# One pair of weights loaded in two parts: 128 rows without the last query tile, and that tile as 64-row tiles in partitions 0 to 63

## The chip, the cores and the metric

The kernel runs on one core of a Trainium2 chip. A core has five engines (TensorE, written PE; VectorE, DVE; ScalarE, ACT; GpSimd, POOL; SyncE, SP), an on-chip memory of 128 partitions, a matmul accumulator memory, and 16 DMA engines that bring data from the chip's main memory. The metric is device microseconds of one execution. The kernel before took 2490.28 us, the median of three runs between 2489.77 and 2490.39.

## The reference

Two layers, each of one attention block over a cached sequence and one token mixer, for a batch of two with one token each. Only float32 is used.

```python
x = x + A(layernorm(x)); x = x + B(layernorm(x))      # twice
def A(x):                        # x: (2, 1, 512)
    q = (x @ wq)                 # 32 query heads of 128, four to each of the 8 key heads
    scores = q . k_cache / sqrt(128)      # k_cache, v_cache: (2, 8, 32768, 128)
    return softmax(scores) @ v_cache @ wo # wo: (4096, 512)
def B(x):                        # (2, 1, 512), one token: outer products
    return gelu(x * w1 + b1) @ w2 + b2    # w1: (1, 1792), w2: (1792, 1)
```

Both caches, 268 MB each, are read once per layer, all but a few pieces that stay on the chip from one layer to the next. The weights wq and wo, 8.4 MB each, are read in head groups.

## The kernel before, in words

**Units.** A unit is one layer, one batch element and one key head: 2 x 2 x 8 = 32 units. For a unit the kernel computes the query rows of the head (`make_q`, `q_products`), loads the head's keys and multiplies them (`load_k`, `k_chunk`, L426), takes the maximum and the exponentials, loads the values and multiplies them (`load_v`, `v_chunk`, L581), and adds the result times wo (`out_0` to `out_2`). A unit's keys and values are 16 MB each, in eight chunks of 4096 positions.

**Memory.** `mem` is one on-chip tile of 13 cells of 4096 columns (2 MB over 128 partitions) and a rest of 2560 columns. In the first and the last part of the program keys and values use cells 0 to 7 as two buffers of four cells, so nearly every load is 8 MB, 128 rows of 64 KB. In the middle (from unit N1 to N3, where one layer ends and the next begins) loads are smaller and use a ring that reaches to cell 10. Cell 8 (`RING * RING - 1`) holds small work rows: `spot()` hands out one of its eight places of 512 columns, in rotation. Cells 9 to 12 hold weights.

**Weights.** Heads go in pairs (`TWO_HEADS`): (0, 1), (2, 3), (4, 6), (5, 7). `load_weights` (L114 to L118) brings a pair by one load of 4096 KB, 128 rows of 32 KB, on SyncE's queue, into cells 9 and 10 or 11 and 12. A head's part is four query tiles (`wq_at`, 128 rows x 512 columns each, one for each quarter of the 512 inputs) and four output tiles (`wo_at`). The pairs that are not resident are loaded once in each layer, seven loads in all. `q_products` (L340) makes the query row of a head as four products of 128 inputs each, `q_ps[n] += xnT[:, d, b].T @ wq_at(h)[:, d, :]`, d = 0 to 3.

**Order.** One loop at the end walks through the loads in the order of `stream`; after each chunk it runs what has been booked for that moment with `at(time, f, ...)`, where time counts chunks. The program order of each engine follows from this. All large loads are issued by SyncE, one after the other; each waits until TensorE has used what stood in its buffer. `at(kbeg[n] - 10, load_weights, ...)` books a pair's load ten chunks before the keys of its first head begin.

Of the kernel before, what the change touches and what calls it, by code (L numbers as in the profile page):

```python
# [13 lines left out]
P = 128  # L14
CK = 4096
# [5 lines left out]
RING = 3  # L21
# [23 lines left out]
def gqa_mixer_kernel(ctx: ExitStack, tc: tile.TileContext, x, kt, v, wqo, cols, out):  # L45
# [17 lines left out]
    nc = tc.nc  # L63
    B, D = out.shape
# [4 lines left out]
    R = wqo.shape[2] // (4 * D)  # L69
    DT = D // P  # L70
    FT = (cols.shape[1] - 1) // 4
# [16 lines left out]
    widths |= dict(selh=R, mask=QT, others=B, oz=2 * R * B, qpads=NP, unit=2 * 16, ln=16 + 2 * FT)  # L88
# [20 lines left out]
    def wq_at(h):  # L109
        return cells(home[h])[:, :W].rearrange("p (t c) -> p t c", t=DT)  # L110

    def wo_at(h):
        return cells(home[h])[:, W:].rearrange("p (t c) -> p t c", t=R)

    def load_weights(k, cell):
        for j in range(2):
            home[TWO_HEADS[k][j]] = cell + j
        nc.sync.dma_start(cells(cell, 2), wqo[k])  # L118


    busy = [0] * 2 * (WCELL0 + WCELLS + 1)
    now = [0]
# [72 lines left out]
    ident = sm["ident"]  # L195
# [84 lines left out]
    N1 = len(units) - 1  # L280
# [5 lines left out]
    N3 = len(units) - 1  # L286
# [7 lines left out]
    xnT = sm["xn"].rearrange("p (d b) -> p d b", b=B)  # L294
# [26 lines left out]
    def unit_of(n):  # L321

        return units[n]

    q_ps, q_row, q_kept = {}, {}, {}
# [7 lines left out]
    def q_products(n, *ds):  # L333

        layer, b, h = unit_of(n)
        m = 1 if partner(n) is None else B
        for d in ds:
            if d == 0:
                q_ps[n] = bcast if N1 < n <= N3 + 2 else kept[0]
            nc.tensor.matmul(  # L340
                q_ps[n][:m, :],
                xnT[:, d, b : b + m],
                wq_at(h)[:, d, :],
                start=(d == 0),
                stop=(d == DT - 1),
            )

    def make_q(n, step, place=None):

# [339 lines left out]
    ln = sm["ln"]  # L689
# [238 lines left out]
    kbeg, k_done, vbeg, v_done, vend_of, v_from, v_to, brings, starts, t = {}, {}, {}, {}, {}, {}, {}, [], [], 0  # L928
# [13 lines left out]
    def at(time, f, *a, rank=1):  # L942
        done.setdefault(time, []).append((rank, f, a))

    HC = NCH // HALVES
    opens = {two[0]: k for k, two in enumerate(TWO_HEADS)}
    mixed = {}
    for n in range(NU):
        layer, b, h = unit_of(n)
# [19 lines left out]
                assert max(v_done[n - 2, c] for c in range(HC)) <= q2  # L969
        if n and h in opens and (units[n] == (0, 0, h) or h in passing and units[n] == (1, 0, h)):  # L970
            at(kbeg[n] - (7 if n == N3 + 2 else 10), load_weights, opens[h], WCELL0 + opens[h] % 2 * 2)
        if n in (N1 + 1, N2 + 1):
            at(kend - 0.5, turn_scores, n, 0, rank=2)
            at(kend, q_products, n + 1, 0)
            at(kend, max_1, n)
            at(kend, q_products, n + 1, 1)
            at(kend, max_2, n)
            at(kend, exponentials_at_once, n, 0)
            at(kend, q_products, n + 1, 2, 3)
            t1 = kend + 2  # L980
# [94 lines left out]
    t = 0  # L1075
# [11 lines left out]
    assert not done, sorted(done)  # L1087


def _layout(A_x, A_k_cache, A_v_cache, A_wq, A_wo, B_w1, B_b1, B_w2, B_b2):  # L1090
# [23 lines left out]
    return {  # L1114
        "x": np.ascontiguousarray(A_x.reshape(B * (D // P), P).T),
        "kt": kt,
        "v": A_v_cache.reshape(B * HKV, SK * DH),
        "wqo": np.stack([np.concatenate([wqo[h] for h in two], axis=1) for two in TWO_HEADS]),
        "cols": np.concatenate(cols, axis=1),
    }  # L1120

# [24 lines left out]
```

## Time and profile before

| | |
|---|---|
| median of three runs | 2490.28 us |
| the profiled execution | 2490.09 us |
| its span | 2488.0 us |
| bytes read | 1061.19 MB |
| granted TensorE clock | 0.772 |
| loads of weight pairs (L118) | 7 of 4096 KB |

The profile has one execution. Its span runs from the first to the last instruction that the profiler saw, 2.1 us less than the execution's own time. Lines L114 and so on are those of the kernel before; in the changed kernel the same statements stand 7 to 44 lines further down.

### The profile page before, as it was taken

To read this page: it belongs to the slowest core of one execution; us is meant where nothing else is said; L and a number is where in the kernel's file an instruction comes from. 1 tells how busy PE (TensorE), PEld (TensorE's weight loads), DVE (VectorE), ACT (ScalarE), POOL (GpSimd) and SP (SyncE) were. 2 spreads that over 40 slices of the span, in tenths; PEclk is the share of its full clock that TensorE was granted. 3 is DMA by queue.
4 is the path that set the end of the run, shared out by engine and by line. 5 is a ranking of instruction groups with operands and counts; after the bars stand their busy time and mean duration, and the time that the engine had idled before them with its cause. 6 is when DMAs were issued, how large, how long until landed. Compare 5 with 4: busy or idle time off the path is not lost.

```text
span 2488.0 us, 20543 instructions
## 1 busy us (share of the span) xinstructions
PE 1371.4 (55%) x9302; PEld 376.2 (15%) x9302; DVE 244.9 (10%) x643; ACT 187.7 (8%) x554; POOL 4.9 (0%) x17
## 2 busy tenths in 40 slices
PE   4544445544545454657677665455455465455546
PEld 1111111111111111111121121111111111111112
DVE  1000000000000000003113110000000000010002
ACT  0000000000000000002012000000000000011002
POOL 0000000000000000000000000000000000000000
PEclk8777767876777777778888887777678677777878
DMA  9999999999999999999999999999999999999996
GB/s 421 437 432 428 433 436 430 434 435 427 436 436 432 426 436 431 427 431 407 433 427 417 428 432 432 438 430 431 432 428 438 428 429 435 431 434 431 432 431 291
DMA packets 30336, 1062.51 MB, mean 427 GB/s; under 512 B 3621, under 2 KB 3625, under 8 KB 4266
## 3 DMA queue, kind: packets, MB, share of 16 engines
q1 hardware_dynamic: 29960, 1061.17, 99.1%
q8 instruction: 73, 1.20, 0.2%
q14 instruction: 13, 0.11, 0.0%
q10 hardware_dynamic: 290, 0.04, 0.0%
HBM read 1061.19 MB, written 0.00 MB: 427 GB/s over the span
## 4 chain that ended last, share of the span: by engine, by line
DMA 73%; PE 25%; DVE 1%; issue 0%; another core or an unknown queue 0%; ACT 0%; SPq 0%; POOL 0%; ACTq 0%
DMA mem<-in_v_dram 64%; PE acc L581 20%; DMA mem<-in_kt_dram 9%; PE scores L426 3%; PE small L612 0%; PE small L455 0%; PE small L449 0%; PE bcast L340 0%; ACT S L466 0%; PE small L642 0%; PE kept L246 0%; PE kept L792 0%; PE bcast L672 0%; DVE S L551 0%
## 5 line engine op out<-in xcount | busy, mean ns | idle before, releaser
L426 PE MATMUL scores<-mem,small_sb 128*32 128x512 f32 x4096 | 631.7, 736 | 605.4 <-DMA mem<-in_kt_dram 605.2
L581 PE MATMUL acc<-mem,S 128*16 128x512 f32 x4088 | 596.8, 723 | 457.1 <-DMA mem<-in_v_dram 447.7
L426 PEld LDWEIGHTS scores<-mem,small_sb 128*32 128x32 f32 x4096 | 150.0, 129 | 988.7 <-issue 903.7
L466 ACT ACTIVATE S<-S,small_sb 128x128 f32<-128x128 f32 x240 | 123.4, 517 | 2107.9 <-DVE small_sb L457 1556.9
L581 PEld LDWEIGHTS acc<-mem,S 128*16 128x16 f32 x4088 | 132.6, 109 | 810.8 <-issue 664.4
L441 DVE TENSOR_REDUCE small_sb<-scores 128x1 f32<-128x512 f32 x64 | 44.2, 691 | 819.5 <-PE scores L426 819.5
L461 DVE STREAM_TRANSPOSE S<-scores 128x512 f32<-128x512 f32 x64 | 45.5, 710 | 116.0 <-PE acc L581 116.0
L340 PE MATMUL kept<-mem,small_sb 128*2 128x512 f32 x104 | 51.1, 617 | 1.7 <-DVE small_sb L274 1.7
L466 ACT ACTIVATION_READ_ACCUMULATOR S<-S,small_sb 128x1 f32 x240 | 44.7, 186 | 0.0
L246 PE MATMUL kept<-mem,small_sb 128*1 128x512 f32 (+1 forms) x236 | 42.4, 598 | 2.6 <-ACT mem L835 2.4
L451 DVE TENSOR_REDUCE small_sb<-small 1x4 f32<-1x128 f32 x32 | 8.9, 279 | 277.7 <-PE small L449 277.7
L614 DVE RECIPROCAL small_sb<-small 128x4 f32<-128x4 f32 x32 | 5.9, 185 | 304.6 <-PE small L612 304.6
L623 DVE TENSOR_TENSOR small_sb<-small,small_sb 128x4 f32<-128x4 f32 x31 | 5.1, 164 | 295.8 <-PE small L621 295.8
L551 DVE SCALAR_TENSOR_TENSOR S<-acc,small_sb,S 128x128 f32<-128x128 f32 x93 | 32.6, 351 | 3.3
L835 ACT ACTIVATE S<-bcast,small_sb 128x512 f32<-128x512 f32 x28 | 21.5, 777 | 87.2 <-DVE small_sb L704 85.1
L366 PE MATMUL small<-small_sb,mem 2*128 2x2 f32 x112 | 15.5, 256 | 17.9 <-DVE mem L362 17.9
L549 DVE TENSOR_SCALAR S<-acc,small_sb 128x128 f32<-128x128 f32 x31 | 10.8, 350 | 147.3 <-PE acc L581 147.3
L621 PEld LDWEIGHTS small<-small_sb,S 128*128 128x128 f32 x62 | 12.7, 258 | 48.8 <-issue 41.2
L340 PE MATMUL bcast<-mem,small_sb 128*1 128x512 f32 (+1 forms) x40 | 19.4, 600 | 0.0
L366 PEld LDWEIGHTS small<-small_sb,mem 2*128 2x128 f32 x112 | 14.3, 196 | 30.5 <-DVE mem L362 27.3
L852 DVE SCALAR_TENSOR_TENSOR acc<-S,small_sb,acc 128x512 f32<-128x512 f32 x24 | 18.1, 755 | 2.5
L449 PE MATMUL small<-small_sb 128*1 128x128 f32 x64 | 16.6, 353 | 3.1 <-DVE small_sb L447 3.1
(147 smaller groups left out, 285.3 us busy)
## 6 DMA issues: line engine op xcount, KB each, us to landing
mem<-in_kt_dram SPq DMA_DIRECT2D x14, 4096.0 KB, 22.5
mem<-in_v_dram SPq DMA_DIRECT2D x11, 4096.0 KB, 29.2
mem<-in_wqo_dram SPq DMA_DIRECT2D x7, 4096.0 KB, 37.6
mem<-in_v_dram SPq DMA_DIRECT2D x13, 2048.0 KB, 21.3
mem<-in_kt_dram SPq DMA_DIRECT2D x12, 2048.0 KB, 19.3
mem<-in_kt_dram SPq DMA_DIRECT2D x24, 1024.0 KB, 8.8
mem<-in_v_dram SPq DMA_DIRECT2D x21, 1024.0 KB, 8.8
mem<-in_kt_dram SPq DMA_DIRECT2D x2, 6144.0 KB, 24.2
```

What stands on the lines that cost most here:

```text
L246: nc.tensor.matmul((rows if to is None else to)[32 * g : 32 * g + b + 1, :], weights if b else weights[:, 1:], row, start=to is not None, ...
L340: nc.tensor.matmul(q_ps[n][:m, :], xnT[:, d, b : b + m], wq_at(h)[:, d, :], start=(d == 0), stop=(d == DT - 1),)
L366: nc.tensor.matmul(pt[:, r * m : (r + 1) * m], q_row[n][:m, r * DH : (r + 1) * DH], ident[:m, :m], start=True, stop=True,)
L426: nc.tensor.matmul(sc_ps[n, half][32 * g : 32 * g + 32, :], q, kc[k * NG + g], start=(i == 0 and k == 0), stop=(i == PACK - 1 and k == SUB ...
L441: nc.vector.tensor_reduce(mx[n][:, half : half + 1], sc_ps[n, half], axis=AX.X, op=ALU.max)
L449: nc.tensor.matmul(pm[:1, :P], mxa, ident, start=True, stop=True)
L461: nc.vector.transpose(S[half], sc_ps[n, half])
L466: nc.scalar.activation(s[:, :, h], s[:, :, h], AF.Exp, bias=neg[n][:, h : h + 1], scale=SCALE, accum_out=lsum[n][:, half, h : h + 1],)
L551: nc.vector.scalar_tensor_tensor(t, acc[:, k * DH : (k + 1) * DH], mask[:, k : k + 1], t, op0=ALU.mult, op1=ALU.add)
L581: nc.tensor.matmul(acc[32 * g : 32 * g + R * QT, :], S[half][:, col : col + R * QT], vc[q], start=(c == v_from[n] and q < NG), stop=(c == ...
L835: nc.scalar.activation(hid[key, f], px[key], AF.Gelu_apprx_tanh, bias=shift[key][:, f : f + 1], scale=slope[key][:, f : f + 1],)
L852: nc.vector.scalar_tensor_tensor(h if f == FT - 1 else acc, h, w, acc, op0=ALU.mult, op1=ALU.add)
```

## The change

The pair (4, 6), number 2 of `TWO_HEADS` (`PART = 2`), is loaded in two parts. The host puts the last query tile (d = 3) of both heads apart. What is left, seven tiles for each head, goes by a load of 3584 KB (128 rows of 28 KB) to the same cells as before. The two tiles taken out, 128 rows each, are cut into an upper and a lower half of 64 rows, and the four half tiles (512 KB) go side by side to partitions 0 to 63 of cell 8, by one load of 64 rows of 8 KB on SyncE's queue, booked 28 chunks ahead of the head's keys. Both loads happen once in each layer.

[...] So `lower_input` copies the inputs 64 to 127 of the last quarter to partitions 0 to 63 (a product with half of the identity matrix and a copy by VectorE), and `q_products` makes the last product of heads 4 and 6 as two products of 64 inputs.

Since cell 8 is now used by the half tiles, `spot()` hands out work rows from the rest (five places) ahead of unit N1 and from unit N3 + 4 on, and from cell 8 only between.

```diff
+PART, LOWERED = 2, 1
...
     def load_weights(k, cell):
+        tiles = 2 * (DT + R - LOWERED * (k == PART))
         for j in range(2):
-            home[TWO_HEADS[k][j]] = cell + j
-        nc.sync.dma_start(cells(cell, 2), wqo[k])
+            home[TWO_HEADS[k][j]] = cell * CK + j * (tiles // 2) * D
+        of = wqo[k].rearrange("p c -> (p c)")[: P * tiles * D].rearrange("(p c) -> p c", p=P)
+        nc.sync.dma_start(mem[:, cell * CK :][:, : tiles * D], of)
+
+    def lower_tiles():
+        low = mem[:H, (WCELL0 - 1) * CK :][:, : 4 * LOWERED * D]
+        to = low.rearrange("u (i c) -> u i c", i=2)
+        for j in range(2):
+            lowered[TWO_HEADS[PART][j]] = [[to[:, i, (LOWERED * j + d) * D :][:, :D] for i in range(2)] for d in range(LOWERED)]
+        of = wqo[PART].rearrange("p c -> (p c)")[-H * 4 * LOWERED * D :].rearrange("(u c) -> u c", u=H)
+        nc.sync.dma_start(low, of)
+
+    def lower_input():
+        p = misc()
+        nc.tensor.matmul(p[:H, : LOWERED * B], ident[:, H:], sm["xn"][:, -LOWERED * B :], start=True, stop=True)
+        nc.vector.tensor_copy(sm["low"][:H, :], p[:H, : LOWERED * B])
...
     def spot():
         spots[0] += 1
-        return cells(RING * RING - 1)[:, spots[0] % (CK // D) * D :][:, :D]
+        inside = kbeg[N1] <= now[0] < kbeg[N3 + 4]
+        w, m = ((WCELL0 - 1) * CK, CK // D) if inside else ((WCELL0 + WCELLS) * CK, REST)
+        return mem[:, w + spots[0] % m * D :][:, :D]
...
+            j = d - (DT - LOWERED)
+            if h in lowered and j >= 0:
+                low = sm["low"][:, j * B : (j + 1) * B]
+                pairs = [(x[:H, b : b + m], t) for x, t in zip((xnT[:, d, :], low), lowered[h][j])]
+            else:
+                pairs = [(xnT[:, d, b : b + m], wq_at(h, d))]
...
             at(kbeg[n] - (7 if n == N3 + 2 else 10), load_weights, opens[h], WCELL0 + opens[h] % 2 * 2)
+            if opens[h] == PART:
+                at(kbeg[n] - 28, lower_tiles)
+                at(kbeg[n] - 28, lower_input)
```

SyncE's issues in the first layer, before, from a K load (`in_kt_dram`) to the pair load (`in_wqo_dram`):

```order
L139 DMA mem<-in_kt_dram 128x16384 [waits DMAHW0_49,PE_49]
L139 DMA mem<-in_v_dram 128x16384 [waits DMAHW1_49,PE_49]
L139 DMA mem<-in_kt_dram 128x16384 [waits DMAHW2_49,PE_49]
L139 DMA mem<-in_v_dram 128x16384 [waits DMAHW3_49,PE_49]
L139 DMA mem<-in_kt_dram 128x16384 [waits DMAHW4_49,PE_49]
L139 DMA mem<-in_v_dram 128x16384 [waits DMAHW5_49,PE_49]
L118 DMA mem<-in_wqo_dram 128x8192
```

and the same place in the changed kernel:

```order
L162 DMA mem<-in_kt_dram 128x16384 [waits DMAHW0_49,PE_49]
L135 DMA mem<-in_wqo_dram 64x2048
L162 DMA mem<-in_v_dram 128x16384 [waits DMAHW1_49,PE_49]
L162 DMA mem<-in_kt_dram 128x16384 [waits DMAHW2_49,PE_49]
L162 DMA mem<-in_v_dram 128x16384 [waits DMAHW4_49,PE_49]
L162 DMA mem<-in_kt_dram 128x16384 [waits DMAHW5_49,PE_49]
L162 DMA mem<-in_v_dram 128x16384 [waits DMAHW6_49,PE_49]
L125 DMA mem<-in_wqo_dram 128x7168
```

The 64-row load stands right behind a K load and five loads ahead of the rest of its pair; it waits for nothing, and the order of all other loads is as it was. In the second layer, changed kernel:

```order
L162 DMA mem<-in_kt_dram 128x16384 [waits DMAHW1_49,PE_49]
L135 DMA mem<-in_wqo_dram 64x2048 [waits DVE_49]
L162 DMA mem<-in_v_dram 128x16384 [waits DMAHW2_49,PE_49]
L162 DMA mem<-in_kt_dram 128x16384 [waits DMAHW3_49,PE_49]
L162 DMA mem<-in_v_dram 128x16384 [waits DMAHW5_49,PE_49]
```

Here the 64-row load has a wait of its own, for VectorE, which wrote the last work rows in cell 8.

TensorE's products for the query row of head 4 (L340, of `q_products`) among the K products (L426), before:

```order
L340 MATMUL kept_85<-mem,small_sb 2x512 [waits DMAHW0_49]
L340 MATMUL kept_85<-mem,small_sb 2x512
L426 MATMUL scores<-mem,small_sb 32x512 x8
L340 MATMUL kept_85<-mem,small_sb 2x512 x2
L426 MATMUL scores<-mem,small_sb 32x512 x8
```

and in the changed kernel, where these lines are L372 and L454:

```order
L372 MATMUL kept_85<-mem,small_sb 2x512 [waits DMAHW1_49]
L372 MATMUL kept_85<-mem,small_sb 2x512
L454 MATMUL scores<-mem,small_sb 32x512 x8
L372 MATMUL kept_85<-mem,small_sb 2x512
L372 MATMUL kept_85<-mem,small_sb 2x512 [waits DMAHW3_49]
L372 MATMUL kept_85<-mem,small_sb 2x512
L454 MATMUL scores<-mem,small_sb 32x512 x8
```

The last of the four products has become two, the first of which waits for the 64-row load.

More of the change, by code (lines that the diff above doesn't have):

```diff
@@ L87, in gqa_mixer_kernel @@
     widths = dict(x=B * DT, xn=B * DT, q=KEPT_Q * R, cols=4 * FT + 1, ident=P, one=1, half=1, selg=R * QT)
-    widths |= dict(selh=R, mask=QT, others=B, oz=2 * R * B, qpads=NP, unit=2 * 16, ln=16 + 2 * FT)
+    widths |= dict(selh=R, mask=QT, others=B, oz=2 * R * B, qpads=NP, unit=2 * 16, ln=16 + 2 * FT, low=LOWERED * B)
     small_sb = const.tile([P, sum(widths.values())], F32, name="small_sb")
@@ L107, in cells, with wq_at @@
         return mem[:, k * CK : (k + m) * CK]
-    def wq_at(h):
-        return cells(home[h])[:, :W].rearrange("p (t c) -> p t c", t=DT)
+    H = P // 2
+    lowered = {}
+    def wq_at(h, d):
+        return mem[:, home[h] + d * D :][:, :D]
     def wo_at(h):
-        return cells(home[h])[:, W:].rearrange("p (t c) -> p t c", t=R)
+        w = home[h] + (DT - LOWERED * (h in lowered)) * D
+        return mem[:, w : w + W].rearrange("p (t c) -> p t c", t=R)
     def load_weights(k, cell):
+        tiles = 2 * (DT + R - LOWERED * (k == PART))
         for j in range(2):
-            home[TWO_HEADS[k][j]] = cell + j
-        nc.sync.dma_start(cells(cell, 2), wqo[k])
+            home[TWO_HEADS[k][j]] = cell * CK + j * (tiles // 2) * D
[12 more added lines that the diff above has]
+        nc.vector.tensor_copy(sm["low"][:H, :], p[:H, : LOWERED * B])
     busy = [0] * 2 * (WCELL0 + WCELLS + 1)
@@ L339, in q_products @@
                 q_ps[n] = bcast if N1 < n <= N3 + 2 else kept[0]
[L340 to L346, printed above, removed]
+            j = d - (DT - LOWERED)
[4 more added lines that the diff above has]
+                pairs = [(xnT[:, d, b : b + m], wq_at(h, d))]
+            for i, (x, t) in enumerate(pairs):
+                nc.tensor.matmul(
+                    q_ps[n][:m, :], x, t, start=(d == 0), stop=(d == DT - 1 and i == len(pairs) - 1)
+                )
     def make_q(n, step, place=None):
@@ L1087, in gqa_mixer_kernel, with _two_heads @@
     assert not done, sorted(done)
+def _two_heads(two, parted, d):
+    import numpy as np
+    if not parted:
+        return np.concatenate(two, axis=1)
+    c = np.arange((d // P - LOWERED) * d, d // P * d)
+    main = np.concatenate([np.delete(a, c, axis=1) for a in two], axis=1)
+    top = [np.concatenate([a[u : u + P // 2, c] for a in two], axis=1) for u in (0, P // 2)]
+    top = np.concatenate(top, axis=1)
+    return np.concatenate([main.ravel(), top.ravel()]).reshape(P, -1)
 def _layout(A_x, A_k_cache, A_v_cache, A_wq, A_wo, B_w1, B_b1, B_w2, B_b2):
@@ L1117, in _layout @@
         "v": A_v_cache.reshape(B * HKV, SK * DH),
-        "wqo": np.stack([np.concatenate([wqo[h] for h in two], axis=1) for two in TWO_HEADS]),
+        "wqo": np.stack([_two_heads([wqo[h] for h in two], k == PART, D) for k, two in enumerate(TWO_HEADS)]),
         "cols": np.concatenate(cols, axis=1),
```

## The prediction

> **What bounds the kernel now.** I read the page from the top: the span and the engines, then the DMA queues, then the chain, then the DMA rate by stage.
>
> ```profile
> span 2488.0 us, 20543 instructions
> PE 1371.4 (55%) x9302; PEld 376.2 (15%) x9302; DVE 244.9 (10%) x643; ACT 187.7 (8%) x554; POOL 4.9 (0%) x17
> ...
> q1 hardware_dynamic: 29960, 1061.17, 99.1%
> q8 instruction: 73, 1.20, 0.2%
> ...
> DMA 73%; PE 25%; DVE 1%; issue 0%; another core or an unknown queue 0%; ACT 0%; SPq 0%; POOL 0%; ACTq 0%
> ```
>
> No compute engine is busy for more than 55%. SyncE's queue q1 keeps the 16 DMA engines busy for 99.1% of the span, so the time is bytes over rate. The chain's 25% on PE are waits for a buffer to come free; the next rows show that the engines have other loads in hand meanwhile. Windows of the span (columns: us, busy time of each engine, TensorE clock, DMA share, GB/s):
>
> ```profile
> 0.00:926.00 926.00, 460.10 (x3128) 126.08 (x3132) 65.21 (x190) 48.50 (x177) 1.65 (x11) 0.76 1.00 432
> 926.00:1440.00 514.00, 335.46 (x2196) 89.49 (x2192) 88.17 (x201) 54.62 (x130) 2.16 (x4) 0.82 1.00 425
> 1440.00:2460.00 1020.00, 555.62 (x3726) 151.62 (x3722) 81.10 (x226) 76.99 (x239) 0.54 (x1) 0.76 1.00 432
> ```
>
> Both pair loads that change lie in the first and the third window: DMA share 1.00, 432 GB/s. An 8 MB load (128 rows of 64 KB, 8.39e6 bytes) takes 8.39/0.432 = 19.4 us. The chain around the place where the second 64-row load will stand, and SyncE's issues there:
>
> ```profile
> 1761.50 38.74 DMA mem<-in_v_dram
> ...
> 1809.80 29.15 DMA mem<-in_v_dram
> ```
>
> ```profile
> 1761.50 0.33 SPq L139 DMA_DIRECT2D mem<-in_v_dram  x1
> 1794.39 0.33 SPq L139 DMA_DIRECT2D mem<-in_kt_dram  x1
> 1809.80 0.33 SPq L139 DMA_DIRECT2D mem<-in_v_dram  x1
> ...
> 1904.88 0.33 SPq L118 DMA_DIRECT2D mem<-in_wqo_dram  x1
> ```
>
> The load issued at 1809.80 lands after 29.15 us, though its own bytes need 19.4. So 9.7 us of earlier loads were still ahead of it; that is the queue's usual reserve. It is thinnest before 1794.39, where the load of 1761.50 lands at 1800.24 and the next is issued 5.85 us before that.
>
> The end of the stream shows a second thing (40 slices of 1 us from 2440 to 2480):
>
> ```profile
> DMA  7999979695999998899988999995443000000000
> GB/s 328 524 393 459 393 328 524 262 590 229 393 426 459 459 459 360 360 442 410 459 377 369 418 430 403 383 367 240 193 188 123 16 0 0 0 0 0 0 0 0
> ```
>
> After 2467 the busy share falls to 5, 4, 4, 3 tenths: about half of the engines have finished, the others work some 4 us longer, and the kernel waits for these (the chain's last load lands at 2471.43). The trace's packet records say the same. For each load, the moment when each of the 16 engines finishes, in us after the first:
>
> ```
> load's first finish (record's clock, 10.5 us ahead of the span's)   1st  8th  9th  16th
>   61.80                                                              0   0.22 0.23 0.54
>  942.64                                                              0   2.17 4.50 6.17
> 1806.01                                                              0   1.57 2.81 4.73
> 2457.62                                                              0   1.38 2.89 4.62
> ```
>
> Where a q8 record (73 instruction fetches of 16 KB, about 1.1 us each) can be followed to its engine, that is one of the last seven in 57 of 60 cases: 73 x 1.1 / 8 = 10 us of extra work on each late engine. The early eight lose that time, partly by waiting; the late eight have the next packet right behind the last all the way. **So the time is the work of the eight late engines**, plus what stands ahead of and behind the stream. A microsecond more or less on them is a microsecond of the kernel.
>
> **The change, part by part**, against the profiled execution's own 2490.09 us (inside the range of the runs shown and 0.19 below their median, 2490.28, so nothing is added for that).
>
> ```profile
> mem<-in_wqo_dram SPq DMA_DIRECT2D x7, 4096.0 KB, 37.6
> ```
>
> *Bytes.* Seven pair loads of 4096 KB; two become 3584 KB of 128 rows and 512 KB of 64 rows. The sum of bytes is the same. The 128-row part falls by 4.194 - 3.670 = 0.524 MB: at 432 GB/s -1.21 us for each of the two, -2.43 in all.
>
> *The 64-row load.* No 64-row load is in the trace, so its price has two ends. If all 16 engines carry four rows each at the usual rate, it is 0.524/432 = +1.21 us, and the change is nil. The other end: whatever 64 partitions receive in this trace they receive as one half of a 128-row load, at 432/2 = 216 GB/s. At that rate the 512 KB take +2.43 us, however many engines share them. I take this end: it is the only rate into 64 partitions that a row shows, and each engine's 8 KB rows would have to share the way into partitions 0 to 63 with the engines that are writing there already. Net per load +2.43 - 1.21 = +1.21 us, for the late engines too, since they carry half of the rows. The lower end, nil, stays in the range.
>
> [...]
>
> *SyncE.* Two issues more, 0.33 to 0.43 us each like those above. By the order of its instructions the second 64-row load follows the K load of 1794.39 and precedes the V load of 1809.80, 15 us in which SyncE only waits; the first has the same place one layer earlier. So it takes no time from another issue: nothing. It waits there for VectorE, for work rows that were last written over two units (two times 38.8 us) earlier: nothing. The V load and all later ones queue behind it; such a wait would cost from the point where it outlasts the 19.4 us of the K load just issued.
>
> *TensorE, VectorE.* Four products more of 512 columns (two heads, two layers) and two small ones with a copy:
>
> ```profile
> L340 PE MATMUL kept<-mem,small_sb 128*2 128x512 f32 x104 | 51.1, 617 | 1.7 <-DVE small_sb L274 1.7
> L366 PE MATMUL small<-small_sb,mem 2*128 2x2 f32 x112 | 15.5, 256 | 17.9 <-DVE mem L362 17.9
> ...
> L374 DVE COPY small_sb<-small 128x4 f32<-128x4 f32 x18 | 3.0, 164 | 26.4 <-PE small L366 26.4
> ```
>
> A product counts as two records, so 51.1/52 = 1.0 us each, 4 us in all, 2 us in any one unit; the small ones about 0.3, the copies 0.16. They stand between K chunks, ahead of a wait like this one:
>
> ```profile
> 314.72 3.64 PE L426 MATMUL scores<-mem,small_sb 128*32 128x512 f32 x16 [10.13 <-DMA mem<-in_kt_dram]
> ```
>
> TensorE idles 10.13 us there. The two extra microseconds can push that unit's buffer release, which eats 2 of the 9.7 us of reserve: nothing. Without the reserve they would cost 2 us per layer.
>
> *Work rows.* Outside the middle units they rotate over five places instead of eight, in another cell. A row is read within a chunk of its writing, so five are enough: nothing. In the middle stage a K load no longer waits for such rows and a 1280 KB V load does, on rows written units earlier: nothing.
>
> **Sum:** 2490.09 - 2.43 + 4.86 = **2492.5 us**, +0.1%.
>
> **Rivals.**
>
> *No cost into one half* (the change does nothing). The way into partitions 0 to 63 has room for all 16 engines: 2490.1. For it: the early engines have idle time to give, and no row proves a limit per half. Against it: no row shows 64 partitions taking more than 216.
>
> *Only the early engines carry it.* If who carries a row goes by its partition, eight engines take eight rows each, and if these are the early eight, the late ones are freed of 1.21 us per load: 2490.09 - 2.43 = 2487.7. The early engines would get 1.21 us more, against the 2.89 us that still part the 8th from the 9th at the end: the late ones stay last. For it: the tail row splits the engines into halves, as partitions would. Against it: if the late eight are the ones that serve partitions 0 to 63, the sign turns and it is 2492.5 again; and the last store, of four rows, left four completion records, as a split by count of rows does. [...]
>
> *Rows wait for rows* (slower). If two engines that share the way into one half take turns by whole rows and not by small pieces, each 8 KB row of a late engine waits for a 64 KB row of its neighbour, 65,536 B at 432/16 = 27 GB/s, 2.43 us; four rows make 9.7 us per load, 19.4 in all: 2509.5. It decides from 2.5 us per load on (0.2% is 5.0 us). Against it: nothing in the trace shows engines taking turns; for it: an instruction fetch of 16 KB costs a late engine 1.1 us where its bytes need 0.6.
>
> **How the numbers follow.** Half rate 0.56 (2492.5), no cost 0.18 (2490.1), early engines 0.17 (2487.7), rows wait 0.06 (2509.5), anything else 0.03, shared by both sides. The first two hold only 0.74, so the range takes in the third: 2487.2 to 2493.4, with 0.5 us below and 0.9 above for what runs differ by and for the small terms; that holds 0.91. A measurement of this kernel can tell about 0.2%, 5 us, from no change. Faster than 2485.3 by none of the named cases: 0.02; slower than 2495.3 by the last and half of the rest: 0.07; within: 0.91.
>
> **What would show it.** In the changed profile: 3584 KB and 512 KB rows for in_wqo, q1's megabytes unchanged, and the DMA share still 1.00 around the two 64-row loads, which should pass some 25 us after the K loads ahead of them are issued (the second near 1820). If the half rate holds, the GB/s there dip for about 2.4 us by half and the 8192-byte records of the new load last twice as long. If only the early engines carry it, there are eight rows on each and the tail after 2467 is shorter by 2.4 us. If rows wait, the spread of the finishing moments jumps by several us at the new load. Wrong would be all of this if SyncE's issue after the new load came late and the DMA share fell below 0.9 there.

## The result and the profile after

The changed kernel took **2502.22 us**, median of five runs (2501.47 to 2503.81); the kernel before took 2490.39 us beside it (five runs, 2489.77 to 2493.09). The ratio is 1.0045, with a 95% interval of 1.0034 to 1.0056: slower, by 11.8 us, where the prediction had 2.4 us. The profiled execution took 2501.79 us against 2490.09, and these 11.7 us are what has to be found.

From the page of the changed kernel: span, engines, the DMA rate in 40 slices of 62.5 us, the queues, the chain.

```profile
span 2499.6 us, 20570 instructions
PE 1382.3 (55%) x9314; PEld 375.2 (15%) x9314; DVE 245.0 (10%) x645; ACT 188.0 (8%) x554; POOL 4.9 (0%) x17
...
DMA  9999999999999999999999999999999999999996
GB/s 419 436 434 428 438 431 433 404 432 434 434 425 425 434 434 433 426 430 409 432 427 415 430 427 438 431 432 436 431 397 430 431 429 435 433 432 431 433 437 280
...
q1 hardware_dynamic: 30120, 1061.17, 99.1%
q8 instruction: 73, 1.20, 0.2%
...
DMA 73%; PE 25%; DVE 0%; another core or an unknown queue 0%; issue 0%; ACT 0%; SPq 0%; ACTq 0%
```

Bytes, q1's share of 99.1% and the chain's shares are as before, to a per cent; the compute engines' busy time is nearly so (TensorE 1382.3 us instead of 1371.4). The DMA engines look just as busy over a span that is 11.6 us longer, so the same bytes went more slowly. Two slices outside the middle stage stand out in the GB/s line, the 8th with 404 and the 30th with 397. They hold the two 64-row loads, which SyncE issued without losing time to a wait (L162 is the line that loads keys and values, L135 the 64-row load):

```profile
445.88 0.33 SPq L162 DMA_DIRECT2D mem<-in_kt_dram  x1
446.26 0.56 SPq L135 DMA_DIRECT2D mem<-in_wqo_dram  x1
461.29 0.33 SPq L162 DMA_DIRECT2D mem<-in_v_dram  x1
```

```profile
1798.65 0.33 SPq L162 DMA_DIRECT2D mem<-in_kt_dram  x1
1799.03 0.48 SPq L135 DMA_DIRECT2D mem<-in_wqo_dram  x1
1816.13 0.34 SPq L162 DMA_DIRECT2D mem<-in_v_dram  x1
```

Both go out 0.4 us after a K load and 15 to 17 us ahead of a V load. Now the stretches in which they move, by windows, first of the kernel before and then of the changed one (columns as in the prediction; the last three are TensorE's clock, the DMA share and GB/s):

```profile
466.00:480.00 14.00, 8.96 (x62) 2.55 (x66) 0.16 (x1) 0.00 (x0) 0.00 (x0) 0.64 1.01 435
1819.00:1835.00 16.00, 10.50 (x74) 2.79 (x74) 1.64 (x4) 2.11 (x8) 0.00 (x0) 0.82 1.00 431
```

```profile
466.00:480.00 14.00, 6.17 (x34) 1.80 (x38) 0.17 (x1) 0.00 (x0) 0.00 (x0) 0.53 1.02 314
1819.00:1835.00 16.00, 4.58 (x26) 1.37 (x30) 0.16 (x1) 0.00 (x0) 0.00 (x0) 0.57 1.00 287
```

The DMA share stays at 1.00 while the rate falls from 433 to 314 and 287. At the mean of 433 this is 14 x (433 - 314)/433 = 3.8 us of lost transfer time and 16 x (433 - 287)/433 = 5.4 us. The trace's packet records, added up by microseconds, show the shape of it (a low row is an 8 KB row of a 64-row load):

```
GB/s in each 1 us (record's clock, 11.3 us ahead of the span's in this run)
first load,  from  478:  387 297 253 239 235 230 236 230 252 292 363 419 433
second load, from 1831:  395 338 255 246 225 224 222 206 199 212 235 270 324 414
8 KB records (64 of each load, 4 on each of 16 engines): median 0.55 and 0.62 us
64 KB records of the neighbouring loads meanwhile:       up to 5.6 us; median of all 2.42
first low row begins to last one ends:  478.4 to 487.1 (8.7 us);  1831.9 to 1843.2 (11.3 us)
```

Added up the same way, these come to 4.1 and 5.3 us, **9.4 of the 11.7**. The loads are slow for far longer than their own 2.4 us at half rate. For the whole time in which any engine has a low row in hand, the 64 KB rows of the K and V loads on the other engines take longer too, up to 5.6 us against the median of 2.42.

In the chain, the V load issued next to each of them lands late: 34.87 us after its issue instead of the 28.93 that it took at this place before, and 35.88 instead of 29.15. First the row of the kernel before for the first place, then the two of the changed one:

```profile
461.31 28.93 DMA mem<-in_v_dram
```

```profile
461.29 34.87 DMA mem<-in_v_dram
...
1816.13 35.88 DMA mem<-in_v_dram
```

What is left, some 2.3 us, is spread out. The last microseconds of the stream (40 slices of 1 us from 2448) show one piece:

```profile
DMA  9999797993966999989999989999974441000000
GB/s 459 393 524 459 328 590 328 393 524 164 688 295 295 393 459 426 524 360 393 393 410 459 393 344 442 418 385 410 375 320 195 199 178 59 18 16 0 0 0 0
```

The half-busy tail is there as before. In the packet records, the 16 engines now end 5.7 us apart instead of 4.62: 1.1 us. About 1 us more goes in a dry spell near 775, where the engines ran short of loads (by the packet records busy for 0.66 and 0.81 of two microseconds); the kernel before has such a spell elsewhere (0.81 and 0.67 near 1146), so not all of it counts. These two were not tested.

### The profile page after: what moved, and what is told of

Its sections match the earlier page's. It is cut to its first block, busy times and chain, and to the rows that moved or that the text cites. A ratio compares the mean times of both kernels' runs of the same rounds, so it can differ in the third digit from the quotient of the medians.

```text
span 2499.6 us, 20570 instructions
## 1 busy us (share of the span) xinstructions
PE 1382.3 (55%) x9314; PEld 375.2 (15%) x9314; DVE 245.0 (10%) x645; ACT 188.0 (8%) x554; POOL 4.9 (0%) x17
## 3 DMA queue, kind: packets, MB, share of 16 engines
q1 hardware_dynamic: 30120, 1061.17, 99.1%
## 4 chain that ended last, share of the span: by engine, by line
DMA 73%; PE 25%; DVE 0%; another core or an unknown queue 0%; issue 0%; ACT 0%; SPq 0%; ACTq 0%
DMA mem<-in_v_dram 64%; PE acc L609 20%; DMA mem<-in_kt_dram 9%; PE scores L454 3%; PE small L483 0%; PE small L640 0%; PE small L670 0%; ACT S L494 0%; ACT mem L842 0%; PE small L477 0%; PE kept L269 0%; PE bcast L269 0%; PE bcast L724 0%; PE bcast L700 0%
## 5 line engine op out<-in xcount | busy, mean ns | idle before, releaser
L454 PE MATMUL scores<-mem,small_sb 128*32 128x512 f32 x4096 | 621.2, 728 | 597.6 <-DMA mem<-in_kt_dram 597.6
L609 PE MATMUL acc<-mem,S 128*16 128x512 f32 x4088 | 611.2, 738 | 465.6 <-DMA mem<-in_v_dram 460.1
L454 PEld LDWEIGHTS scores<-mem,small_sb 128*32 128x32 f32 x4096 | 148.1, 127 | 982.8 <-issue 894.4
L372 PE MATMUL kept<-mem,small_sb 128*2 128x512 f32 (+1 forms) x112 | 54.7, 613 | 1.7 <-DVE small_sb L297 1.7
L372 PE MATMUL bcast<-mem,small_sb 128*1 128x512 f32 (+1 forms) x40 | 20.3, 623 | 0.0
L649 PEld LDWEIGHTS small<-small_sb,S 128*128 128x128 f32 x62 | 11.7, 237 | 47.6 <-issue 40.0
```

Source lines behind the costliest of these rows:

```text
L372: nc.tensor.matmul(q_ps[n][:m, :], x, t, start=(d == 0), stop=(d == DT - 1 and i == len(pairs) - 1))
L454: nc.tensor.matmul(sc_ps[n, half][32 * g : 32 * g + 32, :], q, kc[k * NG + g], start=(i == 0 and k == 0), stop=(i == PACK - 1 and k == SUB ...
L609: nc.tensor.matmul(acc[32 * g : 32 * g + R * QT, :], S[half][:, col : col + R * QT], vc[q], start=(c == v_from[n] and q < NG), stop=(c == ...
```

## The experiments

The theory after this profile: rows that go to one half of the partitions slow the traffic of all engines. Its rivals: the split itself costs (one more load, moved work rows, a thinner reserve); the cause is the size of the rows or the solid block of 64 partitions; only some engines slow, and the kernel waits for these. The diffs are against the changed kernel. The medians of before on the chips used were 2491.80 us (e1 to e4), 2491.03 (e5 to e8), 2491.10 (e9, e10) and 2490.33 (e11).

### e1: the same 64 rows, to every second partition

```diff
-        low = mem[:H, (WCELL0 - 1) * CK :][:, : 4 * LOWERED * D]
-        to = low.rearrange("u (i c) -> u i c", i=2)
+        low = mem[::2, (WCELL0 - 1) * CK :][:, : 4 * LOWERED * D]
+        to = mem[:H, home[TWO_HEADS[0][0]] :][:, : 4 * LOWERED * D].rearrange("u (i c) -> u i c", i=2)
```

> The 64-row load of 512 KB goes to every second partition (0, 2, ... 126) instead of 0 to 63; bytes, rows and order are the same. The last query product of heads 4 and 6 reads other resident weights instead of the tile, so that TensorE's work is the same and only its numbers differ. Theory 'half': rows that all end in one half of the partitions are taken at half the total rate, and everything else on its way meanwhile is slowed with them. Here both halves are reached: no dip of the rate, about 2490.5 us. Rival 'small load': any extra load of 64 short rows does it, whatever its partitions: dips as in the changed kernel (to 200 to 250 GB/s, loss 4.1 and 5.4 us), about 2502.

Measured: 2492.69 us in a single run, 9.1 less than the changed kernel's profiled execution and inside the runs of the kernel before on this chip (2490.29 to 2494.40). Its windows at the two loads:

```profile
466.00:480.00 14.00, 8.83 (x66) 2.59 (x70) 0.16 (x1) 0.00 (x0) 0.00 (x0) 0.68 1.00 431
1819.00:1835.00 16.00, 10.68 (x76) 2.96 (x76) 1.51 (x4) 0.78 (x3) 0.00 (x0) 0.76 1.04 449
```

No dip. The 8 KB records take 0.309 to 0.320 us. The same number of rows, of the same size, at the same moment costs nothing that shows if it goes to every second partition: neither the row size nor the count of rows is the cause.

### e2: the split alone, as 128 rows of 4 KB

```diff
-        low = mem[:H, (WCELL0 - 1) * CK :][:, : 4 * LOWERED * D]
+        low = mem[:, (WCELL0 - 1) * CK :][:, : 2 * LOWERED * D]
...
-        of = wqo[PART].rearrange("p c -> (p c)")[-H * 4 * LOWERED * D :].rearrange("(u c) -> u c", u=H)
+        of = wqo[PART].rearrange("p c -> (p c)")[-H * 4 * LOWERED * D :].rearrange("(u c) -> u c", u=P)
...
-                at(kbeg[n] - 28, lower_input)
```

> The split of the pair alone: the same 512 KB go to cell 8 as 128 rows of 4 KB, a whole tile for each head, with one product each. Theory 'half': no dip, 2490.5 us, the same as before. Rival 'small load': an extra load of short rows behind an 8 MB load costs by itself: 2500 to 2502. Rival 'work rows': part of the 11.8 us is from the move of the work rows to the rest, which is still in here: up to 2 us above before.

Measured: 2490.68 us, median of ten runs, ratio 0.9996 (0.9986 to 1.0006).

```profile
466.00:480.00 14.00, 8.73 (x65) 2.48 (x69) 0.16 (x1) 0.00 (x0) 0.00 (x0) 0.68 1.00 431
1819.00:1835.00 16.00, 9.97 (x74) 2.64 (x74) 1.64 (x4) 2.11 (x8) 0.00 (x0) 0.82 1.01 437
```

The extra load, the moved work rows and SyncE's issue cost nothing that can be measured. The split products and the input copy, which e2 leaves out, are still in e1 and e7, where the time is that of the kernel before within 0.9 us. So the loss belongs to where the 64 rows go.

### e3: the 64 rows to partitions 64 to 127

```diff
-        low = mem[:H, (WCELL0 - 1) * CK :][:, : 4 * LOWERED * D]
+        low = mem[H:, (WCELL0 - 1) * CK :][:, : 4 * LOWERED * D]
...
-        nc.tensor.matmul(p[:H, : LOWERED * B], ident[:, H:], sm["xn"][:, -LOWERED * B :], start=True, stop=True)
+        nc.tensor.matmul(p[H:, : LOWERED * B], ident[:, :H], sm["xn"][:, -LOWERED * B :], start=True, stop=True)
...
```

> The 64-row load goes to partitions 64 to 127, and the inputs are copied up instead of down. Theory 'half', same for both halves: dips of 4 to 5.5 us, 2501 to 2503 us. Rival 'lower half only' (the late engines, which fetch instructions, serve partitions 0 to 63 and these alone are short): a smaller dip or none, 2490 to 2496.

Measured: 2501.76 us in a single run, 10.0 above the median of before on this chip. By the packet records the two dips cost 4.2 and 4.4 us.

```profile
466.00:480.00 14.00, 4.96 (x26) 1.46 (x30) 0.16 (x1) 0.00 (x0) 0.00 (x0) 0.51 1.02 314
1819.00:1835.00 16.00, 6.24 (x46) 1.85 (x50) 0.16 (x1) 0.00 (x0) 0.00 (x0) 0.68 1.02 321
```

Either half does it, so it isn't that the lower half is special.

### e4: eight loads of eight rows, one behind the other

```diff
-        nc.sync.dma_start(low, of)
+        for o in (0, 1, 2, 3, 32, 33, 34, 35):
+            nc.sync.dma_start(low[o : o + 29 : 4, :], of[o : o + 29 : 4, :])
```

> The same 64 rows to partitions 0 to 63, but by eight loads of eight rows, each four partitions apart. Eight rows can be on eight engines only. Theory 'half' with the loss made where engines of both halves push into one: if the eight engines are those that write these partitions in any load, nothing is shared, no dip; if these are also the early engines, the late ones are freed of 1.2 us per pair: 2488 us; if they are the late ones, 2492.9. Rival 'only the partitions count': any rows into one half slow everything, dips as in the changed kernel, 2500 or more. Rival 'small load': sixteen small loads, worse than 2502.

Measured: 2497.29 us (ten runs), ratio 1.0021 (1.0011 to 1.0030). Of its timeline, SyncE's issues (start, busy us):

```profile
444.49 0.33 SPq L163 DMA_DIRECT2D mem<-in_kt_dram  x1
444.87 26.86 SPq L136 DMA_DIRECT2D mem<-in_wqo_dram  x8
471.83 0.38 SPq L163 DMA_DIRECT2D mem<-in_v_dram  x1
```

and the DMA share and rate from 466 to 480 (40 slices of 0.35 us):

```profile
DMA  8802797542221000003995000000994000499400
GB/s 374 374 23 117 304 492 328 211 187 117 117 94 70 0 0 0 0 0 94 468 2434 187 0 0 0 0 0 0 2247 562 187 0 0 0 187 2060 562 187 0 0
```

SyncE's waits on the line of the eight loads (L136), over both layers: us in total, times, longest:

```profile
SPq L136 <- DMA mem<-in_kt_dram: 37.4, 2, 18.7
SPq L136 <- DMA mem<-in_v_dram: 6.1, 2, 3.3
```

Here the time went another way. From the first of the eight issues to the end of the last it is 26.86 us, but each issue takes only 0.62 to 0.78; the rest is waiting. The loads on SyncE's queue count their completion on eight semaphores in turn, as the issues in the trace show (in the changed kernel 214 issues, 26 or 27 on each). Six of the eight small loads go out at once; the seventh waits for the V load and the eighth for the K load that use the same semaphore, the latter for 18.7 us. So the V load behind them came 10 us late, and the engines ran dry: busy share 0. The 8 KB records themselves take 0.31 us in the median, although all 64 rows go to partitions 0 to 63. That was the surprise: the same partitions, without the slow rate.

### e5: the eight loads booked two chunks apart

```diff
-                at(kbeg[n] - 28, lower_tiles)
+                for i, o in enumerate((0, 1, 2, 3, 32, 33, 34, 35)):
+                    at(kbeg[n] - 28 + 2 * i, lower_tiles, o)
```

> The eight loads of eight rows again, but two chunks apart instead of all behind one K load, so that SyncE does not wait for one of them while the queue runs empty (in e4 the eight issues took SyncE 26.9 us, and the rate fell to 0 for 2 us). Theory 'early engines carry it, on their own way': no dip, the late engines are freed of 1.2 us per pair: 2488 us against 2490.5. Rival 'eight rows into one half slow the rest': dips remain, 2494 or more. Rival 'the loss of e4 was the issue, and there is no relief': 2490.5.

Measured: 2493.43 us (eleven runs), ratio 1.0010 (1.0001 to 1.0019). Windows around three groups of the loads of the first layer:

```profile
486.00:496.00 10.00, 5.48 (x38) 1.46 (x42) 0.00 (x0) 0.00 (x0) 0.00 (x0) 0.66 1.00 433
508.00:518.00 10.00, 8.13 (x56) 2.40 (x60) 0.00 (x0) 0.00 (x0) 0.00 (x0) 0.69 1.01 437
529.00:539.00 10.00, 9.67 (x64) 2.88 (x68) 0.44 (x2) 2.20 (x8) 0.00 (x0) 0.72 1.00 433
```

No dips and no gain: neither the 2488 us of the theory came nor the dips of the first rival, and the time is 2.9 us above the 2490.5 of the second. With rows put on engines by following each engine's chain of records, eight engines carry eight rows of each pair. The instruction fetches go to eight engines in strict rotation, and of these only two are among the eight carriers. So the carriers are not "the early eight". On the two that do both, a pair costs 2.43 (eight rows at 432/16 = 27 GB/s) - 1.21 us more, an estimate. Two pairs make 2 x 1.21 = 2.4 us, just what the median lies above before; but the trace does not bear this account out, as e6 shows.

### e6: two tiles of each head instead of one, as in e5

```diff
-PART, LOWERED = 2, 1
+PART, LOWERED = 2, 2
```

> The same with two query tiles of each head (rows of 16 KB, 1 MB a pair). If the early engines carry them, the late ones are freed of 2.4 us per pair, 4.85 in all: 2485.6 us. The early engines get as much, and had about 10 us less to do, so they should not become the late ones. Rival: the gap between the halves is closed before the end, and the gain stops at about 3 us, 2487.5.

Measured: 2497.51 us (nine runs), ratio 1.0026 (1.0016 to 1.0036). A miss of 12 us, on the wrong side. By the account of e5 the two doubly used engines would make 4.9 of these 6.5 us. The packet records of the profiled executions say where the time went: how much later than in the kernel before the first so many MB have landed (us, counted from the moment when 5 MB had). The small loads move between 200 and 245 MB and between 775 and 820 MB.

```
MB landed    150    190    250    300    450    550    760    800   1061
changed      0.0    0.0    4.5    4.2    5.4    5.8    6.3   10.7   10.7
e2          -0.1    0.1    0.4    0.3    0.2    1.2    1.2    0.8    0.4
e5          -0.1   -0.1    0.8    1.1    0.3    4.0    5.1    4.1    4.5
e6           0.1    0.2    0.4    3.2    3.2    3.9    5.6    5.4    5.7
```

The changed kernel falls back by 4.5 and 4.4 us just where its two loads are. e5 and e6 do not: e5's profiled execution (2495.65 us, the slowest of its eleven) loses 3.7 us between 450 and 550 MB, in the middle stage, and e6 2.8 us between 250 and 300 MB, most of it in one dry spell, in which the engines are at worst busy for half of the time. Engines that merely finish last would show behind the last MB: that is 1.1 us in e5 and 1.0 in e6, where the account has 2.4 and 4.9. So what e5 and e6 lose is mostly dry spells and the middle stage, and why they have more of them was not tested.

### e7: a solid block of 64 partitions, 32 to 95

```diff
-        low = mem[:H, (WCELL0 - 1) * CK :][:, : 4 * LOWERED * D]
+        low = mem[32 : 32 + H, (WCELL0 - 1) * CK :][:, : 4 * LOWERED * D]
...
```

> 64 rows to partitions 32 to 95: as many rows side by side as in the changed kernel, but half of them in either half. The last query product of heads 4 and 6 reads other resident weights, as in e1. Theory 'one half is short': no dip, 2490 to 2493 us. Rival 'a solid block of 64 partitions, or rows that land away from where their engine writes otherwise': dips as in the changed kernel or some half of them, 2495 to 2502.

Measured: 2491.59 us in a single run.

```profile
466.00:480.00 14.00, 8.72 (x62) 2.53 (x66) 0.16 (x1) 0.00 (x0) 0.00 (x0) 0.66 0.99 426
1819.00:1835.00 16.00, 11.43 (x76) 3.12 (x76) 1.51 (x4) 0.97 (x4) 0.00 (x0) 0.74 0.99 425
```

No dip worth the name. The solid block over 32 to 95 left the stream at 426 and 425 GB/s; those that fill one half had 314 and 287 (the changed kernel) and 314 and 321 (e3).

### e8: five more 64-row loads, at other moments and of two sizes

```diff
+    def extra_rows(w):
+        src = wqo[0].rearrange("p c -> (p c)")[: H * w].rearrange("(u c) -> u c", u=H)
+        nc.sync.dma_start(mem[:H, (WCELL0 - 1) * CK + 4 * D :][:, :w], src)
...
+    for time, w in ((4, 4 * D), (36, 4 * D), (68, 2 * D), (132, 4 * D), (164, 2 * D)):
+        at(time, extra_rows, w)
```

> The changed kernel with five more 64-row loads to partitions 0 to 63 that nobody reads, in the first layer, 8 KB rows behind chunks 4, 36 and 132 and 4 KB rows behind chunks 68 and 164. Theory 'the loss lasts from the first engine that has such rows to the last': the engines are spread by 0.6 us near the start, 2 us until 360, 3.5 later, and 0.9 x (spread + the rows' own time) gives 1.7, 2.9, 2.4, 4.5 and 4 us, beside their bytes (1.2 or 0.6 us each): about 2521 us in all. Rival 'the loss goes by the bytes': 4.2 us for each load of 8 KB rows, 2.1 for 4 KB, whatever the time: 2523 us, with the first as dear as the others.

Measured: 2521.84 us in a single run. The windows around the load at chunk 4 and around the first layer's changed load:

```profile
30.00:40.00 10.00, 6.94 (x40) 1.98 (x44) 0.00 (x0) 0.00 (x0) 0.00 (x0) 0.56 1.01 367
...
476.00:490.00 14.00, 4.80 (x26) 1.47 (x30) 0.16 (x1) 0.00 (x0) 0.00 (x0) 0.52 0.97 290
```

The same load loses 1.5 us at the one place and 4.2 at the other. By the packet records, beside how far apart the engines' finishing moments were just before:

```
engines apart (us)   0.55   2.12   3.37   4.53 (the changed load)  |  2.98   4.8
rows                 8 KB   8 KB   8 KB   8 KB                     |  4 KB   4 KB
lost (us)            1.54   3.66   2.12   4.24                     |  1.66   2.27
```

The loss is smallest where the engines are in step, and at a like spread 4 KB rows lose less than 8 KB rows (2.27 us at 4.8 apart, against 4.24 at 4.53). The spread alone does not order it: the third column has more of it than the second and loses less, although in both 12 or 13 of the 16 engines are within 0.9 us of each other. Neither of the two formulas expected, by the spread plus the rows' own time or by the bytes alone, gives all six. That the total came out at the 2521 us of the first is luck: the five added loads lost 11.3 us in their dips, where it had 15.5.

### e9: who is slowed? Eight-row loads as marks

Three extra 64-row loads, and around them five loads of eight 6 KB rows. A 6 KB record in an engine's chain tells that it is one of the eight that carry eight-row loads.

```diff
+    def eight_rows():
+        src = wqo[0].rearrange("p c -> (p c)")[: 8 * 3 * D].rearrange("(u c) -> u c", u=8)
+        nc.sync.dma_start(mem[0:29:4, (WCELL0 - 1) * CK + 4 * D :][:, : 3 * D], src)
...
+    for time in (4, 36, 68):
+        at(time, extra_rows)
+    for time in (12, 32, 64, 96, 108):
+        at(time, eight_rows)
```

> The changed kernel with three more 64-row loads to partitions 0 to 63 in the first layer (behind chunks 4, 36 and 68, nobody reads them) and, beside these and the changed one, loads of eight rows that mark the eight engines which carry them; in e4 such rows went at full rate, so these engines write partitions 0 to 63 in any load. Theory 'way into the half': while other engines bring in rows of a 64-row load, the 64 KB rows of the marked engines are slowed and those of the unmarked eight are not. Rival 'everything': the 64 KB rows of both groups are slowed alike, as the total rate in the changed kernel suggests (225 to 250 of 433 GB/s). In both the loss is 1.5 us at the start, where the engines are 0.6 us apart, and 3 to 4.5 us later; about 2518 us in all.

That the marked engines write partitions 0 to 63 in any load is the author's inference from the 0.31 us rows of e4; no record tells which partition an engine writes.

Measured: 2515.28 us in a single run. At the load near 200 us on the record's clock the slowest 64 KB row of each marked engine takes 4.3 to 5.3 us, that of each unmarked one 4.3 to 5.1, against a median of 2.42 in the whole run. Both groups carry low rows, and both are slowed alike. It isn't that one half of the engines stands in a queue while the other goes on.

### e10: the first layer's load moved to where the engines are in step

```diff
-                at(kbeg[n] - 28, lower_tiles)
+                at(kbeg[n] - 28 if layer else 4, lower_tiles)
```

> The changed kernel, but in the first layer the 64-row load goes behind chunk 4, near the start, where the 16 engines are within 0.6 us of each other; in the second layer it stays. Theory 'the loss grows with the distance of the engines': 1.5 us instead of 4.1 for this load (the value of e8 at that place), 2499.5 us against 2502. Rival 'the loss goes with the load, wherever it is': 2502.

Measured: 2497.92 us (nine runs), ratio 1.0026 (1.0015 to 1.0036).

```profile
30.00:40.00 10.00, 6.84 (x44) 2.03 (x48) 0.00 (x0) 0.00 (x0) 0.00 (x0) 0.61 1.02 367
466.00:480.00 14.00, 5.97 (x38) 1.80 (x42) 0.16 (x1) 0.00 (x0) 0.00 (x0) 0.63 1.00 431
1814.00:1830.00 16.00, 5.43 (x26) 1.58 (x30) 0.16 (x1) 0.00 (x0) 0.00 (x0) 0.57 0.97 303
```

Moved to the start, the load loses 1.62 us instead of 4.1, and the old place shows its full 431 GB/s; in the second layer, where it stays, it still loses 4.2. The kernel is 4.3 us faster than the changed one (2502.22, other chip), where 2.5 follow from the load itself. The other 1.8 us are not accounted for.

### e11: e5 with the eight-row loads sent to the other half

Eight loads of eight rows in each layer, two chunks apart as in e5, but to partitions 64 to 127.

```diff
-        low = mem[:H, (WCELL0 - 1) * CK :][:, : 4 * LOWERED * D]
+        low = mem[H:, (WCELL0 - 1) * CK :][:, : 4 * LOWERED * D]
...
-        nc.sync.dma_start(low, of)
+        nc.sync.dma_start(low[o : o + 29 : 4, :], of[o : o + 29 : 4, :])
...
```

> [...] The last query product of heads 4 and 6 reads other resident weights, as in e1. Theory 'an engine that writes into the other half slows all': the 8 KB records take 0.45 us and more instead of 0.31, the rate dips at each of the eight loads, and the time is 2496 to 2503 us. Rival 'only a load that sends all 16 engines into one half at once does it': rows of 0.31 us, no dips, 2493 us as e5.

Measured: 2504.56 us in a single run, 14.2 above the one run of before on this chip and 11.1 more than e5 on another.

```profile
486.00:496.00 10.00, 3.25 (x16) 0.76 (x20) 0.15 (x1) 0.00 (x0) 0.00 (x0) 0.51 0.97 360
508.00:518.00 10.00, 4.31 (x28) 1.32 (x32) 0.00 (x0) 0.00 (x0) 0.00 (x0) 0.56 0.94 347
529.00:539.00 10.00, 3.89 (x22) 1.13 (x26) 0.00 (x0) 0.00 (x0) 0.00 (x0) 0.50 0.97 360
```

Each place where e5 has 433 to 437 GB/s now dips. The packet records have 1.3 to 1.5 us lost at each of the six groups of two loads and 0.5 to 0.6 at each of the four single ones, 10.9 us in all. From 470 to 575 us, 189 of the 64 KB records take more than 2.5 us; in e5 it is 3. The theory's dips are there, but the time is above its range, and the 8 KB rows slow down less than expected: medians of 0.37 to 0.41 us in the groups and 0.31 in the single loads, where 0.45 and more was expected. Most of the price is paid by the rows of other loads.

Are the carriers the same engines as in e5? If they went by partition, they would be the other eight, and (as long as the same engines fetch instructions in both runs) six of the eight that fetch would be among them instead of two. Followed by their chains in the second layer, the fetches at 1804.3 and 1843.8 us fall on carriers and those at 1719.4, 1758.3, 1884.9, 1905.5 and 1946.1 do not; the eighth is unclear. The two are neighbours in the rotation, as in e5. So the carriers seem to be the same eight in both runs, and the same loads go to one half without a dip (433 to 437 GB/s in e5) and to the other at this price (347 to 360 here). It isn't "64 partitions" as such.

## Why the prediction was wrong, point by point

**What bounds the kernel: right.** The bytes' rate bounds it, before and after; the two loads changed the rate, and by that 9.4 of the 11.7 us.

***Bytes*: right.** q1 moves the same 1061 MB, and the 28 KB rows of the shorter pair load take 1.065 us where 32 KB rows take 1.215: with eight rows on each engine 1.2 us less.

***The 64-row load*: the step that failed.** The prediction took "+2.43 - 1.21 = +1.21 us" per load: half rate for the load's own 512 KB. The half rate is real, as are the four rows on each engine and the marks named for it (8192-byte records that last twice as long, GB/s halved at a DMA share of 1.00). But measured were losses of 4.1 and 5.3 us. The term was mis-sized, because it let all other traffic pass untouched. In fact the K and V rows in flight are slowed like the low rows (up to 5.6 us instead of 2.42, and medians of 0.55 and 0.62 instead of 0.31), for as long as any engine has a low row in hand. That is not 2.4 but 8.7 and 11.3 us, since the engines come to the load up to 4.6 us apart, and those still ahead of it are slowed on their way to it. The mirror test is e1 and e7, where the rows go to both halves and all of it is gone.

The 216 GB/s behind the term were an estimate from 432/2, and no run shows them as the limit of one half. As a price for the kernel it falls short: 2.4 us less the load's own bytes leave 1.2, and 4.1 and 5.3 were lost. And e5 writes into 0 to 63 at 0.31 us per 8 KB row with no dip (433 to 437 GB/s), so the half alone isn't the cause in a busy stream.

What the eleven kernels show is this: **64 rows into one half alone, or loads of eight rows into 64 to 127, slow the whole stream; 64 rows over both halves, or loads of eight rows into 0 to 63, do not.** The 64 rows, four on each engine in the changed kernel, cost 4.1 and 5.3 us into 0 to 63 and 4.2 and 4.4 into 64 to 127 (e3); into 32 to 95 (e7, 426 and 425 GB/s) and into every second partition (e1, 431 and 449) there was no dip. The loads of eight rows, on eight engines, kept 433 to 437 GB/s into 0 to 63 (e5) and had 347 to 360 into 64 to 127 (e11).

What ties an engine to a half is not shown. That an engine has a half that it writes freely, and that its rows for the other slow the stream, is the author's conjecture from e5 against e11, where the carriers seem to be the same eight; no row gives an engine's number or the partitions that it writes.

***SyncE*, *TensorE, VectorE*, *Work rows*: right at nothing.** e2 keeps all but the input copy and the split products, at 0.9996; e1 and e7 keep those too (12 matmul records more, 9314 against 9302). What a wait in SyncE's queue can cost was seen only in e4.

**The late eight engines.** "A microsecond more on them is a microsecond of the kernel" is not borne out: by the account of e5 two of them got 2.4 us more there and 4.9 in e6, and behind the last MB only 1.1 and 1.0 were lost. Of the eight that carry eight-row loads and the eight that fetch, two are the same (e5). So the rival *Only the early engines carry it* was wrong twice: sixteen carry, and where only eight do (e5), there is no gain.

***Rows wait for rows*: nearer in time, wrong in mechanism.** It allowed for the slowing of one transfer by another, with 19.4 us against 11.7. But it had one 8 KB row wait for one 64 KB row; the records show low rows at 0.55 to 0.62 us, none above 0.97, and the whole stream at about half of its 433 GB/s (230 and 199 at the lowest). As a case in which the load slows other traffic it deserved more than 0.06: the row of instruction fetches, 1.1 us for 0.6 us of bytes, had already shown traffic that costs more than its bytes.

**The range** ended at 2493.4. It took "half rate" as the dearest likely case because it priced the load in isolation. The bound from the other side was at hand: the load lives in a stream, and if all of it goes at half rate while any engine has low rows, the loss is half of the time from the first engine's first low row to the last engine's last. With the spread of 4.62 us at the end plus 2.4 us of rows, this is 3.5 us per load, 2497; with the 6.17 us seen once in the table, 4.3 us, 2498.7. In the changed kernel half of that time is 4.35 and 5.6 us, beside the 4.1 and 5.3 lost. The record's clock in the prediction's table is ahead by 10.9 us and not 10.5; nothing hangs on it.

**Open.** Why rows for one half slow all 16 engines together: in e9 the slowest 64 KB rows took 4.3 to 5.3 us on the marked engines and 4.3 to 5.1 on the others, and no run shows what they share. Open too: the formula of the loss (e8's third column), the 1 us near 775, and the 2.4 and 6.5 us of e5 and e6.

## What to carry to other kernels

Price a transfer by what it does to the stream that it runs in, not by its own bytes at its own rate: look for a fall of GB/s at a DMA share of 1.0, and for records of *other* loads that take longer. When bytes bound the kernel, keep every load on both halves of the partitions, in one of the forms that were free here (128 rows, or 64 rows over 32 to 95, or every second one); the split itself was free here (e2, 0.9996), the half wasn't (1.0045). No variant tried beats the kernel before.

## What the runs showed of the hardware that was not expected

- 512 KB into one half of the partitions took the whole stream from 433 to about 200 to 250 GB/s for 8.7 and 11.3 us; the same 512 KB over both halves took nothing that shows (431 and 449 GB/s in e1, 426 and 425 in e7).
- Eight engines are enough to cause it, and which half they write decides: 433 to 437 GB/s in e5, 347 to 360 in e11.
- The price depends on the moment: 1.5 to 1.6 us where the engines are in step (e8, e10), 4.1 and 5.3 us where they are 3.5 and 4.6 us apart (the changed kernel); e8 has 2.1 us at 3.4 apart.
- A load of fewer rows took SyncE longer to issue: 0.33 to 0.43 us for 128 rows, 0.48 to 0.56 for 64, 0.62 to 0.77 for eight (e5).
- Instruction fetches rotate over the same eight engines, every eighth to the same one, and two of these eight are among the eight that carry eight-row loads (e5).
